# Threshold attention and a bilinear feed-forward layer on one core: the turned weights cross DRAM by head and partition

## The chip, the cores and the metric

The kernel runs on one core of one Trainium2 chip. The metric is the device time of an execution in microseconds. A core has five engines, each with its own instruction stream: TensorE (PE in the profile) multiplies matrices and writes to PSUM, VectorE (DVE) and ScalarE (ACT) do the elementwise work, GpSimd (POOL) does more of it on SBUF alone, and SyncE (SP) issues DMA transfers. Sixteen DMA engines carry the transfers between DRAM and SBUF; SBUF has 128 partitions.

## The reference

Attention first, for 8 batches and 8 heads, 576 positions, 64 features per head, all in fp32:

```python
scores = np.matmul(q, k.transpose(0, 1, 3, 2)) / sqrt(64)
thresh = np.max(scores, axis=-1, keepdims=True) - tau
scores = np.where(scores >= thresh, scores, -1e9)
attn = softmax of scores along the keys          # written out with max, exp, sum
x = np.matmul(attn, v)                           # then (B, H, S, D) -> (B*S, H*D) = (4608, 512)
out = ((x @ w_a) * (x @ w_b)) @ w_out            # d_ff = 1536
```

So a weight of a query is nonzero only where its score lies within tau of the maximum of its row. The weights are multiplied with v, and for that product the keys must lie on the partitions, whereas the softmax needs the queries on the partitions. The kernel therefore has to turn every matrix of weights.

## The kernel before

**Tiling.** Work is done in pairs of heads (32 pairs, index `i`, four pairs to a batch) and units (index `u`): units 0 to 3 hold 128 queries each for both heads of the pair, unit 4 holds the last 64 queries of two neighbouring pairs. There are 144 units. One turn of the outer loop, called a slot below, starts one unit and moves earlier ones along: scores (line 404, PE), maximum and threshold (411, 412, DVE), exponential (432, ACT), mask and sum (435, DVE), normalising (454, ACT), turning, and three slots after its scores the product with v (542, PE).

**Turning.** The first eight units are turned on PE. All others go through DRAM. `turn_blocks` lets DVE transpose the tile `tw`, 128 queries by 2 heads by 576 keys, in blocks of 32 by 32 (line 498, one instruction for each head, 128x576). After that, partition g\*32+p of `tw` holds key p of each of the 18 key blocks, for the 32 queries of group g. The block groups still have to move to other partitions, and four DMAs per unit, one for each group g of 32 partitions, write them to a DRAM scratch tile `swap` (runs of 1,152 bytes, 144 KB each). One slot later `turn_back` reads `swap` into the tile `wT` with two DMAs of 288 KB, each for two of the groups and all 128 partitions, in runs of 1,152 bytes. A unit 4 has eight writes of 72 KB. The product (`weighted`, `product`) then multiplies `wT` with `vm`, the rows of v: partition by partition, slot s by slot s, so that v must be laid out over partitions and slots as the keys of `wT` are.

**Loads of v.** `load_v` brings v of one pair. For pairs from the second batch on it posts four DMAs of 72 KB, each to 32 partitions. For the first four pairs v is loaded at the start in one order and once more, with `again`, in the order that the turned weights need.

**Order of the work.** The order on every engine is fixed when the program is written. The feed-forward layer (lines 720 and 824 for the two input products, 885 and 935 for the output) is a generator whose matmuls fill the slots; `advance` takes a number of columns from it, and how much each slot takes follows from the backlog. All these transfers are issued by SP, in order, each behind the waits of those ahead of it. Up to slot 36 `post` issues a transfer at once (line 144). From then on it is put into a list, `bulk`, the transfers of turned weights ahead of recent loads. `passed` takes entries from that list as PE's columns go by (320 columns for each 144 KB) and issues them at line 157; the first move of such an entry waits for the PE instruction last written before it. `flush` issues, without that wait, everything up to an entry that is about to be needed. `load_weights` (line 271) brings the weights of the layer in the first 120 us.

Three buffers hold `tw` (`TW_BUFS`), five scratch tiles in DRAM each hold `swap` for units 0 to 3 and for unit 4, and `wT` has two buffers of one unit each (`bufs=2`), so that a read into `wT` has to wait until the product before the last has used its buffer.

Of the kernel before, what the change touches and what calls it, by code (L numbers as in the profile page):

```python
# [10 lines left out]
FP32 = mybir.dt.float32  # L11
# [43 lines left out]
def kernel(  # L55
# [39 lines left out]
    B, H, S, D = q.shape  # L95
    P = 128
    Q = 32
    DM = H * D
    DFF = w_a.shape[1]
    HP = H // 2  # L100
    NT = 4
# [3 lines left out]
    NB = S // Q  # L105
# [6 lines left out]
    NSLOT = 9  # L112
    G = P // Q
# [4 lines left out]
    def pool(name, bufs, **kw):  # L118
        return ctx.enter_context(tc.tile_pool(name=name, bufs=bufs, **kw))
# [5 lines left out]
    scratch = pool("scratch", 5, space=bass.MemoryType.DRAM)  # L125
# [9 lines left out]
    loaded = {}  # L135
# [3 lines left out]
    def post(key, *moves):  # L139

        if not state["paced"]:
            for move in moves:
                state["turn"] += state["over"]
                (nc.scalar if state["turn"] % 2 else nc.sync).dma_start(*move)  # L144
        else:
            at = len(bulk)
            if key[0] in ("tw", "wT"):
                while at and bulk[at - 1][0][0] not in ("tw", "wT") and bulk[at - 1][1] >= state["slot"] - 1:
                    at -= 1
            bulk.insert(at, (key, state["slot"], moves))  # L150
# [13 lines left out]
    def flush(*keys):  # L164

        while any(key in keys for key, _, _ in bulk):
            pump(1, False)
# [33 lines left out]
    def load_v(i, again=False):  # L201
        b, hp = pairs[i]
        if not again:
            loaded[i]["v"] = loads.tile([P, NSLOT, D], FP32, tag="vm", bufs=HP, name="vm")
        for j in range(2):
            rows, half = v[b, 2 * hp + j], loaded[i]["v"][j * D:(j + 1) * D]
            if i >= HP or again:
                if i < HP:
                    rows = rows.rearrange("(c s p) d -> p c s d", c=2, p=Q)
                else:  # L210
                    rows = rows.rearrange("(p c s) d -> p c s d", c=2, p=Q)
                post(("v", i), *((half[c * Q:(c + 1) * Q], rows[:, c]) for c in range(2)))
            else:
                nc.sync.dma_start(half, rows.rearrange("(s p) d -> p s d", p=D))

# [10 lines left out]
    for f in range(NG):  # L226
        for c in range(HP):
            for dst, w in ((wa_sb, w_a), (wb_sb, w_b)):
                src = []
                for r in range(2):  # L230
                    chunks = [(2 * c + e) % HP * 2 + (r + (c >= HP // 2)) % 2 for e in range(2)]
                    cols = slice(f * CW + r * CH, f * CW + (r + 1) * CH)
                    rows = w[:, cols].bitcast(U32).rearrange("(k p) f -> p k f", p=D)
# [98 lines left out]
    for _ in range(TW_BUFS):  # L332
        t = work.tile([P, 2 * NB, Q], FP32, tag="tw", bufs=TW_BUFS, name="rows")
# [10 lines left out]
    load_rows(2, "k", rooms[5])  # L344
    load_weights(RAWS)
    load_v(0)
    load_rows(3, "q", rooms[6])
    load_rows(3, "k", rooms[7])
# [6 lines left out]
    prepared, scored, weights, turned, whole = {}, {}, {}, {}, {}  # L355
    x_of, xtail_of = {}, {}
    ahead, settled, settled_of = {}, {}, {}
    blocks, complete, swaps = [], [], {}
# [106 lines left out]
    def turned_tile():  # L465
        return work.tile([P, G + 1, NSLOT, Q], FP32, tag="wT", bufs=2, name="wT")
# [26 lines left out]
    def turn_blocks(i, u):  # L493

        ws, _ = weights.pop((i, u))
        t = whole.pop((i, u))
        for w in ws:
            nc.vector.transpose(w, w)  # L498
        swap = scratch.tile([G, P, NSLOT * Q], FP32, tag="swap" if u < NT else "swapt", name="swap")
        swaps[i, u] = swap  # L500
        for g in range(G):
            if u < NT:
                moves = [(swap[g].rearrange("(r p) e -> p r e", p=Q),
                          t[g * Q:(g + 1) * Q].rearrange("p (r s) e -> p r (s e)", r=G))]
            else:
                moves = []
                for m in range(2):
                    j = g // 2 ^ m
                    moves.append((swap[2 * m + g % 2, j * D:(j + 1) * D].rearrange("(r p) e -> p r e", p=Q),
                                  t[g * Q:(g + 1) * Q, m * NB:(m + 1) * NB].rearrange("p (r s) e -> p r (s e)", r=2)))  # L510
            post(("tw", i, u), *moves)

    def turn_back(i, u):

        key = "wT", i, min(u // 2, 1) if i >= HP else u // 2
        if u < NT or i < HP:
            flush(("tw", i, u))
            swap = swaps.pop((i, u)).rearrange("g p e -> p g e")
            turned[i, u] = turned_tile()
            for y in range(0, G, 2):  # L520
                post(key, (turned[i, u][:, y:y + 2].rearrange("p g s e -> p g (s e)"), swap[:, y:y + 2]))
        if i >= HP and u == (3 if i % 2 else NT):
            flush(("tw", i - i % 2, NT))
            swap = swaps[i - i % 2, NT].rearrange("g p e -> p g e")
            for y in range(2):
                post(key, (turned[i, 2 + y][:, G].rearrange("p s e -> p (s e)"), swap[:, i % 2 * 2 + y]))
            if i % 2:
                del swaps[i - 1, NT]
# [506 lines left out]
    first = {i: g for g, (i, u) in enumerate(units) if u == 0}  # L1035
# [21 lines left out]
    n = 0  # L1057
# [4 lines left out]
    for g in range(len(units) + PV_LAG):  # L1062
# [9 lines left out]
        if BY_PE + 1 < g <= len(units) + 1:  # L1072
            n = g - PV_LAG
            back = (1 if BY_PE <= n and parts(*units[n]) else 0,)
            if not back[0]:
                turn_back(*units[g - 2])
        if here:
            i, u = units[g]
# [20 lines left out]
        if g > BY_PE and g <= len(units):  # L1099
            turn_blocks(*units[g - 1])  # L1100
# [19 lines left out]
        if g > BY_PE:  # L1120
            n = g - PV_LAG
            held = 0.0
            now = parts(*units[n]) if BY_PE <= n < len(units) else []
            if now:
                held = 384 - (PORTIONS[2] + PORTIONS[3]) * pace + NSLOT * sum(width(*x) for x in now) // 2
                held = min(max(held, 0.0), 384)
            advance(PORTIONS[1] * pace - held)
            for p, h in now:
                if pairs[p][1] == 0:
                    make_x(2 if h == 1 and p >= HP and pairs[p][0] % GT == 0 else 1)  # L1130
                make_room()
                weighted(p, h)
                passed(NSLOT * width(p, h) // 2)
                running["owed"] -= NSLOT * width(p, h) // 2
            if back and back[0] > 0:
                turn_back(*units[g - 2])
# [21 lines left out]
        for p in range(1, NPR):  # L1158
            if g == first[p] - 1:
                load_v(p)  # L1160
        if BY_PE <= g < BY_PE + HP:
            load_v(g - BY_PE, again=True)
# [63 lines left out]
```

## Time and profile before

| | |
|---|---|
| runs, median of 3 | 1419.77 us (1418.38 to 1431.88) |
| profiled execution, span from first to last instruction | 1417.0 us |
| profiled execution, own time | not printed; the fastest run is 1.4 us and the median 2.8 us above the span |
| granted TensorE clock, mean | 0.994 |
| PE busy | 1370.2 us (97%) |
| DVE busy | 1013.7 us (72%) |
| ACT busy | 679.9 us (48%) |
| POOL busy | 495.7 us (35%) |
| SP's DMA queue, all transfers | 323,712 packets, 216.95 MB, 59.2% of 16 engines' time |
| of these, writes of `swap` | 480 of 144 KB (2.9 us to landing), 128 of 72 KB (3.0 us) |
| of these, reads into `wT` | 244 of 288 KB (3.9 us), 56 of 144 KB (3.3 us) |
| of these, loads of `vm` after the start | 128 of 72 KB (2.5 us) |

The busy share of an engine is an average over the whole span. The page also gives the span in forty slices; the trace can be asked for any stretch, for what each engine waited for, and for the chain of work that ended last. "Landing" is the time from SP's issue of a transfer to the semaphore that tells of its last byte. Where the page names a line, it is a line of the kernel printed above; an arrow `wT<-swap` reads "written from".

### The profile page before, as it was taken

The page shows a single profiled execution, that of the slowest core. Times are in us where ns is not written, and L with a number is a line of the kernel's source. Part 1 is how long each engine was busy: PE and PEld are TensorE (multiplying, and loading weights), DVE is VectorE, ACT ScalarE, POOL GpSimd, SP SyncE. Part 2 cuts the span into 40 slices and gives each one's busy share as a digit, 9 for nine tenths or more (in the row PEclk, how much of TensorE's full clock was granted, in tenths as well). Part 3 has the DMA queues.
Part 4 walks back from the last instruction along what each step waited for, and adds up shares of the span by engine and source line. Part 5 has one row for each costly group of instructions (what it writes and reads, how often), then busy time and mean ns, then how long its engine had stood idle before and what let it go on. Part 6 is the DMA issues. An engine that isn't in the chain of part 4 may idle for free.

```text
span 1417.0 us, 76257 instructions
## 1 busy us (share of the span) xinstructions
PE 1370.2 (97%) x33836; PEld 1229.6 (87%) x33836; DVE 1013.7 (72%) x2200; ACT 679.9 (48%) x1245; POOL 495.7 (35%) x678
## 2 busy tenths in 40 slices
PE   6788999999999999999999999999999999999998
PEld 5677579989878887979998999999888899799997
DVE  6898986778777877776767777677777776744424
ACT  5786554545445454545444545454545455431110
POOL 2674541606060606042333324150606060608100
PEclk9999999999999999999999999999999999999999
DMA  9967776667756775666555675567655775550000
GB/s 212 235 193 219 182 214 163 178 153 183 198 135 173 198 188 155 178 156 184 142 134 149 168 193 158 144 160 199 168 144 152 191 201 154 135 152 18 4 19 18
DMA packets 327000, 223.20 MB, mean 158 GB/s; under 512 B 171536, under 2 KB 310800, under 8 KB 326672
## 3 DMA queue, kind: packets, MB, share of 16 engines
q1 hardware_dynamic: 323712, 216.95, 59.2%
q8 instruction: 266, 4.36, 1.3%
q10 hardware_dynamic: 2960, 1.38, 0.4%
q14 instruction: 62, 0.51, 0.1%
HBM read 128.58 MB, written 89.65 MB: 154 GB/s over the span
## 4 chain that ended last, share of the span: by engine, by line
PE 86%; DVE 7%; DMA 3%; issue 2%; SPq 1%; ACT 0%; POOL 0%; DVEq 0%; POOLq 0%; ACTq 0%
PE pab L720 29%; PE po L885 20%; PE pab L824 16%; PE pv L542 10%; PE sc L404 10%; DVE mx L411 2%; DVE tw L498 2%; SPq L144 1%; DMA wT<-swap 1%; DVE tw L435 1%; PE tp L479 1%; DMA raw<-in_moe_w_a_dram 1%; DMA raw<-in_moe_w_b_dram 1%; DVE thr L412 0%; DVE u L790 0%
## 5 line engine op out<-in xcount | busy, mean ns | idle before, releaser
L411 DVE TENSOR_REDUCE mx<-sc 128x1 f32<-128x576 f32 x288 | 204.7, 752 | 125.8 <-PE sc L404 125.4
L454 ACT ACTIVATE tw<-tw,rcp 128x576 f32<-128x576 f32 x272 | 196.5, 770 | 202.3 <-DVE rcp L448 202.3
L682 POOL TENSOR_TENSOR h<-h,u 128x512 f32<-128x512 f32 x28 | 35.2, 1276 | 601.0 <-DVE h L794 426.1
L432 ACT ACTIVATE tw<-sc,bias,scalars 128x576 f32<-128x576 f32 x288 | 239.8, 833 | 10.9 <-PE pab L720 0.4
L435 DVE SCALAR_TENSOR_TENSOR tw<-sc,thr,tw 128x576 f32<-128x576 f32 x288 | 221.5, 799 | 10.4 <-ACT tw L432 9.9
L885 PE MATMUL po<-wo_sb,h 64*64 64x256 f32 x3264 | 205.8, 376 | 1.2 <-DVE h L794 1.1
L498 DVE STREAM_TRANSPOSE tw<-tw 128x576 f32<-128x576 f32 x272 | 194.4, 752 | 0.8 <-ACT tw L454 0.8
L885 PEld LDWEIGHTS po<-wo_sb,h 64*64 64x64 f32 x3264 | 157.0, 133 | 25.7 <-DVE h L794 2.6
L542 PE MATMUL pv<-wT,vm 64*64 64x160 f32 (+3 forms) x5184 | 169.2, 275 | 7.6 <-issue 3.6
L542 PEld LDWEIGHTS pv<-wT,vm 64*64 64x64 f32 x5184 | 157.4, 136 | 19.1 <-issue 9.8
L404 PE MATMUL sc<-kT,qT 64*64 64x288 f32 x2016 | 168.0, 404 | 1.1 <-DVE xt L550 0.5
L853 POOL TENSOR_TENSOR h<-h 128x256 f32<-128x256 f32 x168 | 117.4, 732 | 107.4 <-PE po L885 97.2
L885 PE MATMUL po<-sums_u,h 64*64 64x256 f32 x2448 | 153.4, 376 | 0.7 <-DVE h L832 0.7
L720 PE MATMUL pab<-xU,wb_sb 64*64 64x128 f32 x4352 | 138.0, 269 | 0.4 <-issue 0.3
L720 PEld LDWEIGHTS pab<-xU,wb_sb 64*64 64x64 f32 x4352 | 132.2, 133 | 3.7 <-issue 1.1
L885 PEld LDWEIGHTS po<-sums_u,h 64*64 64x64 f32 x2448 | 117.6, 133 | 19.4 <-DVE h L832 1.3
L404 PEld LDWEIGHTS sc<-kT,qT 64*64 64x64 f32 x2016 | 101.8, 133 | 22.6 <-issue 5.0
L549 ACT COPY xT<-pv 128x128 f32<-128x128 f32 (+1 forms) x68 | 17.7, 260 | 201.8 <-PE pv L542 200.2
L431 ACT ACTIVATE bias<-mx,scalars 128x1 f32<-128x1 f32 x288 | 83.1, 288 | 64.0 <-DVE mx L411 63.7
L550 DVE COPY xT<-pv 64x128 f32<-64x128 f32 (+1 forms) x136 | 38.1, 280 | 91.0 <-PE pv L542 89.7
L720 PE MATMUL pab<-xS,wa_sb 64*64 64x128 f32 x2176 | 101.8, 269 | 0.1
L531 ACT COPY kept<-po 128x512 f32<-128x512 f32 x65 | 34.8, 536 | 123.0 <-PE po L885 113.9
(156 smaller groups left out, 2414.3 us busy)
## 6 DMA issues: line engine op xcount, KB each, us to landing
wT<-swap SPq DMA_DIRECT2D x244, 288.0 KB, 3.9
swap<-tw SPq DMA_DIRECT2D x480, 144.0 KB, 2.9
vm<-in_v_dram SPq DMA_DIRECT2D x128, 72.0 KB, 2.5
swap<-tw SPq DMA_DIRECT2D x128, 72.0 KB, 3.0
kT<-in_k_dram SPq DMA_DIRECT2D x112, 72.0 KB, 3.3
wT<-swap SPq DMA_DIRECT2D x56, 144.0 KB, 3.3
out_dram<-kept SPq DMA_DIRECT2D x28, 256.0 KB, 3.9
qT<-in_q_dram SPq DMA_DIRECT2D x112, 40.0 KB, 2.8
```

Source lines behind the costliest of these rows:

```text
L404: nc.tensor.matmul(sc[m][o * D:o * D + wide, c], qT[r, q0:q0 + wide], kT[r, c * SH:(c + 1) * SH], start=True, stop=True)
L411: nc.vector.tensor_reduce(mx[:, c], sc[j], axis=AX.XY, op=ALU.max)
L431: nc.scalar.activation(bias[:, j:j + 1], mx[:, j:j + 1], AF.Copy, scale=e_nscale)
L432: nc.scalar.activation(wb[j], sb[j], AF.Exp, bias=bias[:, j:j + 1], scale=e_scale)
L435: nc.vector.scalar_tensor_tensor(out=wv, in0=sb[j], scalar=thr[:, j:j + 1], in1=wv, op0=ALU.is_ge, op1=ALU.mult, accum_out=sums[:, j:j + 1])
L454: nc.scalar.activation(w, w, AF.Copy, scale=rcp[:, j:j + 1])
L498: nc.vector.transpose(w, w)
L542: nc.tensor.matmul(pv[c * D:(c + 1) * D, y], vm[rows, s], wT[y](rows, s), start=(s == 0), stop=(s == NSLOT - 1))
L720: nc.tensor.matmul(out[c * D:(c + 1) * D, r, f * P:(f + 1) * P], w[g][k][rows, w0:w0 + D], moving[k][rows], start=(fresh and k == 0 and f ...
L824: nc.tensor.matmul(pab[c:c + columns(), r], w[rows, f // n, k, fs + c:fs + c + columns()], moving, start=(k == 0), stop=(k == H - 1))
L853: (nc.vector if state["over"] else nc.gpsimd).tensor_tensor(*a, **kw)
L885: nc.tensor.matmul(po[c * D:(c + 1) * D, r, y], ht[rows, t0:t0 + D], other[rows, f], start=(f == 0), stop=(f == NF // 2 - 1))
```

## The change

The turned weights of units 0 to 3 are written to DRAM by head: `swap` becomes two blocks of 128 partitions by 576 values, and one DMA for each head writes what each partition holds of that head as one run of 2,304 bytes. Each of the two reads then fetches one head: it fills 64 partitions (head 0 the lower ones, head 1 the upper) for all four groups, still in runs of 1,152 bytes, because the two halves of a partition's run (c = 0 and 1) go to neighbouring partitions. A key that lay on partition c\*32+p of its half now lies on p\*2+c. Unit 4 is written with four DMAs in place of eight, each with two runs of 2,304 bytes for a partition, to places in DRAM that lie interleaved; it is read as before.

The loads of v follow the new order of the keys. For pairs from the second batch on, each partition then needs one run of 2,304 bytes, and the pair is loaded by one DMA of 288 KB over 128 partitions. The second load of the first four pairs keeps its four DMAs, each to every other partition of a half.

```diff
-            if i >= HP or again:
-                if i < HP:
-                    rows = rows.rearrange("(c s p) d -> p c s d", c=2, p=Q)
-                else:
-                    rows = rows.rearrange("(p c s) d -> p c s d", c=2, p=Q)
-                post(("v", i), *((half[c * Q:(c + 1) * Q], rows[:, c]) for c in range(2)))
+            if again:
+                rows = rows.rearrange("(c s p) d -> p c s d", c=2, p=Q)
+                post(("v", i), *((half[c:D:2], rows[:, c]) for c in range(2)))
+            elif i >= HP:
+                if j == 0:
+                    both = v[b, 2 * hp:2 * hp + 2].rearrange("j (q s) d -> (j q) (s d)", s=NSLOT)
+                    post(("v", i), (loaded[i]["v"].rearrange("p s d -> p (s d)"), both))
...
-        swap = scratch.tile([G, P, NSLOT * Q], FP32, tag="swap" if u < NT else "swapt", name="swap")
+        if u < NT:
+            swap = scratch.tile([2, P, S], FP32, tag="swap", name="swap")
+            for j in range(2):
+                post(("tw", i, u), (swap[j], t[:, j * NB:(j + 1) * NB].rearrange("p n e -> p (n e)")))
+        else:
+            swap = scratch.tile([G, P, NSLOT * Q], FP32, tag="swapt", name="swap")
+            rows = swap.rearrange("g (j p c) x -> (g j) p (c x)", j=2, c=2)
+            for g in range(G):
+                first, step = 2 * (g % 2) + g // 2, 5 - 2 * (g // 2)
+                post(("tw", i, u), (rows[first:first + step + 1:step].rearrange("m p x -> p m x"),
+                                    t[g * Q:(g + 1) * Q].rearrange("p (m n) e -> p m (n e)", m=2)))
         swaps[i, u] = swap
-        for g in range(G):
-            if u < NT:
-                moves = [(swap[g].rearrange("(r p) e -> p r e", p=Q),
-                          t[g * Q:(g + 1) * Q].rearrange("p (r s) e -> p r (s e)", r=G))]
-            else:
-                moves = []
-                for m in range(2):
-                    j = g // 2 ^ m
-                    moves.append((swap[2 * m + g % 2, j * D:(j + 1) * D].rearrange("(r p) e -> p r e", p=Q),
-                                  t[g * Q:(g + 1) * Q, m * NB:(m + 1) * NB].rearrange("p (r s) e -> p r (s e)", r=2)))
-            post(("tw", i, u), *moves)
...
-            swap = swaps.pop((i, u)).rearrange("g p e -> p g e")
+            swap = swaps.pop((i, u))
             turned[i, u] = turned_tile()
-            for y in range(0, G, 2):
-                post(key, (turned[i, u][:, y:y + 2].rearrange("p g s e -> p g (s e)"), swap[:, y:y + 2]))
+            for y in range(2):
+                if u < NT:
+                    rows, groups = slice(y * D, (y + 1) * D), slice(0, G)
+                    src = swap[y].rearrange("(g p) (c x) -> (p c) g x", g=G, c=2)
+                else:
+                    rows, groups = slice(0, P), slice(2 * y, 2 * y + 2)
+                    src = swap[groups].rearrange("g p e -> p g e")
+                post(key, (turned[i, u][rows, groups].rearrange("p g s e -> p g (s e)"), src))
```

## The prediction

> **What bounds the kernel now.** I read the page's busy times, slices and chain first, then PE's waits, then stretches of time, and last the transfers one by one.
>
> From the page of before (busy us by engine; the slices of PE and of the DMA engines; the shares of the chain that ended last):
>
> ```profile
> PE 1370.2 (97%) x33836; PEld 1229.6 (87%) x33836; DVE 1013.7 (72%) x2200; ACT 679.9 (48%) x1245; POOL 495.7 (35%) x678
> ...
> PE   6788999999999999999999999999999999999998
> ...
> DMA  9967776667756775666555675567655775550000
> ...
> PE 86%; DVE 7%; DMA 3%; issue 2%; SPq 1%; ACT 0%; POOL 0%; DVEq 0%; POOLq 0%; ACTq 0%
> ```
>
> PE is the bound. It idles for 35.2 us between its first and last matmul (gaps between successive matmuls, added up), of which 18.2 us lie before 100 us, where eight units are turned on PE and no weights cross DRAM until about 91 us. The DMA engines are half to three quarters busy almost throughout, and yet transfers make 3% of the chain. The stretches tell where (start:end, length, then busy us of PE, PEld, DVE, ACT, POOL, the granted clock, DMA share, GB/s):
>
> ```profile
> 100.00:125.00 25.00, 20.11 (x304) 18.51 (x302) 23.60 (x51) 18.32 (x37) 12.64 (x14) 1.00 0.90 263
> 125.00:133.00 8.00, 6.23 (x155) 5.84 (x157) 3.95 (x13) 3.14 (x8) 1.69 (x2) 0.57 0.74 204
> 133.00:200.00 67.00, 65.48 (x1066) 43.50 (x1066) 61.20 (x132) 38.97 (x74) 39.79 (x30) 1.00 0.73 183
> 200.00:1400.00 1200.00, 1191.13 (x30786) 1087.08 (x30782) 839.27 (x1817) 544.21 (x978) 383.38 (x560) 1.00 0.57 151
> ```
>
> From 200 us on PE idles for 8.9 us in 1,200, and no wait on a transfer is among PE's waits there. Between 100 and 200 us it idles for 8.2 us, with the one wait on the turned weights (engine, line, releaser; us in total, times, longest):
>
> ```profile
> PE pv L542 <- DMA wT<-swap: 2.9, 1, 2.9
> ```
>
> That wait ends at 126.8 us. What PE and its clock did around it (length, PE busy, clock, DMA share, GB/s):
>
> ```profile
> 105.40:108.90 3.50, 2.14 (x33) 1.00 1.04 253
> 108.90:112.30 3.40, 2.02 (x36) 1.00 1.04 354
> ...
> 122.50:125.90 3.40, 1.34 (x13) 1.00 0.84 282
> 125.90:129.30 3.40, 2.53 (x96) 0.51 0.70 177
> 129.30:132.80 3.50, 3.50 (x69) 0.51 0.84 229
> ```
>
> After the stretch with 1.34 us of PE work the granted clock is halved for 6.8 us, which costs 3.4 us; after those with 2.14 and 2.02 us it is not. **Everything that faster transfers can give is thus near 120 to 200 us: the 2.9 us, the 3.4 us and some tenths, about 6.5 us or 0.5%.**
>
> **How near the rest is to waiting.** For each of the 64 products from `swap` I subtracted the landing of its last read into `wT` from the start of its first matmul. For those after 200 us this slack is 2.8 to 12.2 us, mostly 4 to 8. For the eight from 126 to 197 us it is -0.6 to 1.4 us (below zero where the first matmuls use a tile read earlier), but for one with 9.0. This is what a slower read eats into.
>
> **SP's issues.** The turned weights in SP's queue (ns min/median/max of an issue, first and last start):
>
> ```profile
> L157 SPq DMA_DIRECT2D swap<-tw x480: 302/393/2142, 324.1 to 1258.5; - x160
> L144 SPq DMA_DIRECT2D swap<-tw x128: 302/432/2436, 91.4 to 314.5; - x128
> ```
>
> Each of the 120 units through DRAM loses two writes (240), each of 16 units 4 loses four (64), each of 28 pairs loses three loads of v (84): 388 of SP's transfers. At 0.39 to 0.43 us each that is 160 us of SP time. From 200 us on SP waits for PE and DVE anyway, so it is worth nothing. From 90 to 200 us SP issues 150 transfers that take 82 us, in runs without a pause; 40 of them go, 17 us. The read PE waits for at 126.8 us is the pair issued at 120.6 and 121.2 us. Before it stand eight unit-4 writes, four loads of v and four writes. The last writes can't start before DVE's transposes (116.3 to 117.8 us), so only what follows counts: two writes and a little, after which the read is issued near 118.6 us, **2.0 us earlier**. Issues before the read landing at 178.8 us fall likewise: three of v, two of writes, 5 x 0.45 = 2.2 us.
>
> **The write.** In the trace's packet records, taken where only one tile's transfers were in flight, a packet of 1,152 bytes took 74.2 ns on average (median 79) when writing `swap` from 32 partitions, and 61.8 ns (median 51) when reading into all 128. A packet of 2,304 bytes from 128 partitions isn't in the trace: at least the 93 ns median of the 2,304-byte packets of `vm`, at most their mean over all, 129 ns (they go to 32 partitions). The nearest row is the store of `out` from 128 partitions, 94.6 ns for 2,048 bytes, thus 106 ns. For a unit: 512 x 74.2 / 16 engines = 2.37 us before, 256 x 106 / 16 = 1.70 us after (1.50 to 2.06), a gain of 0.7 us (0.3 to 0.9). The first head can also go before the second transpose has ended, 0.75 us sooner by the transposes' 754 ns; the unit is complete no sooner.
>
> **The read.** The 61,440 packets keep their size, but fill only half of the partitions at a time. Nearest row: the 74.2 ns of the writes from 32; bounds 61.8 (nothing changes) and 104 (95th percentile of those writes). A pair of reads costs 512 x (74.2 - 61.8) / 16 = 0.40 us more (0 to 1.35). The Trainium skill has a rule against this part: "SBUF — State Buffer", section "Door 1: The DMA port swizzle", says that what counts is how many of 16 ports the partitions reach, and that partitions 0 to 63 reach eight, no more than 0 to 31 do. By it, reads into halves would go at half rate, 32 packets x 51 ns more for each engine and pair, an estimate of 1.6 us from that page's halving and the 51 ns median, and the sum below would come out near nothing; the 79 against 51 ns in this trace agree in direction.
>
> **The sum for the DMA engines**: writes 5,167 us of engine time to 3,690 (69,632 x 74.2 ns against 34,816 x 106), reads up by 762. That is 715 of 22,672 us, three points of share, with bounds of 8 points either way. After 200 us nothing waits for it.
>
> **v.** One load of 288 KB for four of 72 KB: the same bytes, a slot ahead of use. The repeated load has the same packets to every other partition. Both at nothing, hidden by that slot; uncovered, each would cost its landing, 2.5 us. `passed` now takes 288 KB per entry, at 640 columns; the last piece of a unit is taken 320 columns earlier than now. Nothing.
>
> **Sum.** At 126.8 us: 2.0 us sooner by SP, 0.2 to 0.4 later by the read, so the wait falls from 2.9 to about 1.2 us. PE then works for about 3 us instead of 1.34 in 122.5 to 125.9, more than the 2.02 after which the clock stayed: another 3.4 us. That would be 5.1 us. But DVE is busy for 61.2 of the 67 us that follow (91%), so part of it comes back as waits for DVE; and seven thin products lose some tenths. I take **3 us** (bounds: a gain of 6.5; a loss of 7 x 1.35 plus one more halved clock, 3.4, which is 12.9). The profiled span would go from 1417.0 to 1414.0. A span lies 1.4 us under the fastest run and 2.8 under the median, and I carry the difference to the median: 1419.8 - 3 = 1416.8 us.
>
> **Rivals.**
> - *Reads become the bound of the thin stretch*, 0.2 of the chance: SP's gain doesn't reach the reads, since the two `wT` buffers hold them until a product ends, and each read lands up to 1.35 us later. Seven products and one halved clock: 1420 to 1433 us. Against: SP's runs without pause there, in which a read leaves sooner. The rule of the Trainium skill named above leads here.
> - *Slower by over 1%: false order among interleaved writes*, 0.08. The four new writes of a unit 4 go to interleaved blocks of DRAM. If the program orders transfers by the outer bounds of what they touch, each waits for the landing of the one before: 3 x 3.0 us with SP held, against 8 x 0.41 now, 5.7 us more in each of 16 units 4. Reads behind have 3 to 8 us of slack, so 1 to 2 us would reach PE each time, and the repeated loads of v, likewise interleaved, would hold SP 8 x 2.5 us at the thinnest place, of which I count half: 1419.8 + 16 x 1.5 + 10 = 1454 us. It decides once SP is held longer than the slack, about 4 us. Against: in the output product GpSimd (line 853) writes one interleaved half of `h` while PE reads the other with no such wait.
> - *Faster by over 1%*, 0.04: the 8.9 us after 200 us would have to go as well, 1404 us. They are waits on DVE and issue; nothing here touches them.
> - *The traffic doesn't get cheaper* (2,304 bytes cost 129 ns and reads 104): DMA share up by 8 points, hidden by the slack after 200 us. It is part of the first rival.
>
> **Numbers.** The forecast, a gain of 0 to 6.5 us, has 0.68. One per cent, 14.2 us, is about what a measurement of this kernel can tell from no change. Faster 0.04, within 1% 0.88, slower 0.08. The range goes from 1411 (the gain of 6.5 and two for the spread of the runs) to 1433 (the first rival's end).
>
> **What would show it.** Right: the wait at 126.8 us shorter or gone and the clock whole there; writes of 288 KB with packets near 106 ns; reads with packets above 62 ns; PE again idle for under 10 us after 200 us. Wrong: waits of PE line 542 on `wT` after 200 us, several writes of a unit 4 with issues of 3 us, or a clock halved in more places.

## The result and the profile after

The changed kernel takes 1427.94 us (median of 22 runs, 1422.44 to 1433.26) against 1420.79 us before (22 runs, 1414.55 to 1431.88). The ratio is 1.0056, with a 95% interval of 1.0042 to 1.0070: **slower by about 8 us**, where a gain of 3 us was forecast. By the bound of 1% it is "within 1%"; the time lies in the range given. The profiled executions differ by more than the medians: spans of 1430.5 us (own time 1432.69) and 1417.0 us, so that a difference in microseconds between the two traces is up to twice that of a typical pair of runs.

The page of after, with busy times, slices, queues of the DMA engines (packets, MB, share of 16 engines) and the chain:

```profile
PE 1372.3 (96%) x33836; PEld 1210.5 (85%) x33836; DVE 1012.6 (71%) x2200; ACT 678.9 (47%) x1245; POOL 495.4 (35%) x678
...
PE   6788999999999999999999999999999999999998
...
DMA  9967865658547755665546755567546665450000
...
q1 hardware_dynamic: 282688, 216.93, 57.2%
q8 instruction: 266, 4.36, 1.3%
...
PE 85%; DVE 8%; DMA 3%; issue 2%; ACT 1%; SPq 1%; POOL 0%; DVEq 0%; POOLq 0%; ACTq 0%
```

SP's queue has 41,000 packets fewer and two points less of the engines' time, where three were forecast; nothing on this page looks like a loss. The stretches (start:end, length, busy us of PE, PEld, DVE, ACT, POOL, clock, DMA share, GB/s) show where it is:

```profile
100.00:125.00 25.00, 20.42 (x331) 18.86 (x331) 23.61 (x51) 18.26 (x37) 12.63 (x14) 1.00 0.88 258
125.00:133.00 8.00, 7.81 (x182) 7.56 (x176) 7.26 (x19) 6.37 (x15) 3.51 (x5) 1.00 0.86 218
133.00:200.00 67.00, 63.78 (x1076) 42.81 (x1076) 60.80 (x129) 38.30 (x72) 37.82 (x28) 1.00 0.76 197
200.00:1400.00 1200.00, 1181.64 (x30404) 1060.14 (x30400) 825.60 (x1795) 540.35 (x972) 382.76 (x560) 1.00 0.56 150
```

From 125 to 133 us PE is now busy for 7.81 us at full clock, where it had 6.23 us at 0.57. From 200 us on it idles for 18.4 us in place of 8.9. PE's matmuls come in the same order in both kernels, so the n-th matmul of one trace can be set against the n-th of the other: matmul 1,800 is 4.4 us earlier after the change, the 3,000th (at 205 us) 2.7 us earlier, and from there on the changed kernel loses 14.8 us until matmuls at 1300 us, in some twenty jumps of 0.3 to 1.9 us, less what is won back between them.

PE's waits on "issue" from 200 us on (engine, line, releaser; us in total, times, longest), at the same two lines first before, then after. Lines 720 and 726 are the same line of the two kernels, as are 542 and 548:

```profile
PE pab L720 <- issue: 1.2, 3, 0.6
PE pv L542 <- issue: 1.2, 2, 0.7
```

```profile
PE pab L726 <- issue: 9.2, 13, 1.5
PE pv L548 <- issue: 3.1, 6, 0.7
```

"Issue" means that no semaphore ended the wait. No read into `wT` is among the waits of either. The longest one in PE's timeline of after (start, length, what, idle before):

```profile
1127.78 1.11 PE L726 MATMUL pab<-xU,first_u 64*64 64x128 f32 x27
1130.44 1.20 PE L726 MATMUL pab<-xU,first_u 64*64 64x128 f32 x34 [1.54 <-issue]
```

The wait falls between two matmuls of one row of matmuls with the same operands. What it waits for is in the page's third part: queue 8, "instruction", 266 transfers of 16,384 bytes. I numbered PE's records (matmuls, weight loads, its sequencer's waits) in the order of their starts: 68,191 in the changed kernel, which is 266 times 256 with 95 left over. In the changed kernel 14 of PE's gaps over 300 ns from 200 to 1300 us come before a record whose number leaves **193 when divided by 256**, and no other remainder comes more than once; in the kernel before, 3 do, with the same remainder. Each of these gaps ends 1.2 to 1.6 us after a transfer on queue 8 has landed: here it lands at 1128.86 us and PE goes on at 1130.44. So every 256 instructions PE needs the next 16 KB of its program, and in these places it has come too late. I call them the steps of the instruction stream. The idle time of PE at the steps (within two instructions of them, 200 to 1300 us) is 2.2 us before and 12.8 us after; all its other idle time there is 6.6 and 5.5 us.

On average a fetch starts 0.72 us after PE has passed a step in the kernel before, and 1.01 us in the changed kernel; it lands 1.83 and 2.15 us after that step, and nine in ten within 2.74 and 3.39 us. PE needs it for the next step. A row of matmuls of 128 columns runs through 256 instructions in about 3.5 us (27 ns for a matmul and its weight load), and needs the fetch more than 1.2 us before their end. That is the margin: some tenths of a microsecond, for a transfer that the page counts on the same 16 DMA engines (1.3% of their time) as all that SP issues (57.2%). In the changed kernel a fetch that starts while no transfer of SP's is in flight starts 0.39 us after the step; with reads and writes of `swap` in flight, 1.64 us.

### The profile page after: what moved, and what is told of

It is laid out like the page before. It is cut to its first block, busy times and chain, and to the rows that moved or that the text cites. A ratio compares the mean times of both kernels' runs of the same rounds, so it can differ in the third digit from the quotient of the medians.

```text
span 1430.5 us, 75362 instructions
## 1 busy us (share of the span) xinstructions
PE 1372.3 (96%) x33836; PEld 1210.5 (85%) x33836; DVE 1012.6 (71%) x2200; ACT 678.9 (47%) x1245; POOL 495.4 (35%) x678
## 3 DMA queue, kind: packets, MB, share of 16 engines
q1 hardware_dynamic: 282688, 216.93, 57.2%
## 4 chain that ended last, share of the span: by engine, by line
PE 85%; DVE 8%; DMA 3%; issue 2%; ACT 1%; SPq 1%; POOL 0%; DVEq 0%; POOLq 0%; ACTq 0%
PE pab L726 29%; PE po L891 20%; PE pab L830 15%; PE pv L548 10%; PE sc L405 10%; DVE mx L412 2%; DVE tw L499 1%; DVE tw L436 1%; DMA qT<-in_q_dram 1%; PE po L941 1%; DVE low L312 1%; DMA raw<-in_moe_w_b_dram 1%; DVE thr L413 1%; SPq L144 0%; DVE wa_sb L320 0%
## 5 line engine op out<-in xcount | busy, mean ns | idle before, releaser
L891 PEld LDWEIGHTS po<-wo_sb,h 64*64 64x64 f32 x3264 | 151.0, 133 | 32.7 <-DVE h L800 2.5
L891 PEld LDWEIGHTS po<-sums_u,h 64*64 64x64 f32 x2448 | 112.8, 133 | 25.7 <-DVE h L838 1.4
```

The costliest lines, as they stand in the source:

```text
L891: nc.tensor.matmul(po[c * D:(c + 1) * D, r, y], ht[rows, t0:t0 + D], other[rows, f], start=(f == 0), stop=(f == NF // 2 - 1))
```

## The experiments

Theory 1: the reads into half of the partitions hold up the fetches. Its rivals: theory 2, the writes of 288 KB in long runs do; theory 3, the load of v in one piece does. Each kernel was timed against the kernel before on the same chip, and profiled once. "Idle at the steps" is the figure just defined, from that one profile.

**Half reads alone.** In the kernel before, `turn_back`:

```diff
-            for y in range(0, G, 2):
-                post(key, (turned[i, u][:, y:y + 2].rearrange("p g s e -> p g (s e)"), swap[:, y:y + 2]))
+            for y in range(2):
+                if u < NT:
+                    rows = slice(y * D, (y + 1) * D)
+                    post(key, (turned[i, u][rows, 0:G].rearrange("p g s e -> p g (s e)"), swap[rows]))
...
```

> The kernel before, with one part of the change: the two reads of a unit each fill 64 partitions for four groups instead of 128 partitions for two. Writes and loads of v as before. Idle time of PE at the 16 KB steps of its instruction stream, 200 to 1300 us: 2.2 us before, 12.8 us after. Theory 1 (reads into half of the partitions hold up the instruction fetches): 1428 to 1435 us, this idle time 8 to 14 us, reads landing in 4.5 to 5 us. Theory 2 (writes of 288 KB in long runs do it) and theory 3 (the load of v in one piece does it): 1419 to 1423 us, idle time 2 to 4 us.

Measured: ratio 1.0107 (1.0081 to 1.0132), idle at the steps 14.5 us, reads landing in 4.8 us. Theory 1 holds, with idle time and time just above its ranges (the ratio makes 1436 us of the 1420.79), and the reads alone cost more than the whole change. PE's largest wait of this kernel from 200 us on, again at the line of the first feed-forward product:

```profile
PE pab L724 <- issue: 11.8, 19, 1.4
```

**The rest of the change without the half reads.** In the changed kernel:

```diff
-            swap = scratch.tile([2, P, S], FP32, tag="swap", name="swap")
-            for j in range(2):
-                post(("tw", i, u), (swap[j], t[:, j * NB:(j + 1) * NB].rearrange("p n e -> p (n e)")))
+            swap = scratch.tile([G, P, NSLOT * Q], FP32, tag="swap", name="swap")
+            for g in range(G):
+                post(("tw", i, u), (swap[g].rearrange("(j p c) x -> p j (c x)", j=2, c=2),
+                                    t[g * Q:(g + 1) * Q].rearrange("p (j n) e -> p j (n e)", j=2)))
...
-                if u < NT:
-                    rows, groups = slice(y * D, (y + 1) * D), slice(0, G)
...
+                rows, groups = slice(0, P), slice(2 * y, 2 * y + 2)
+                src = swap[groups].rearrange("g p e -> p g e")
```

> The changed kernel, but the four writes of a unit go by group of 32 partitions (144 KB each, runs of 2,304 bytes) and its two reads fill all 128 partitions for two groups, as before. Load of v in one piece, as after. Theory 1 (half reads): 1416 to 1421 us, idle time at the steps of the instruction stream 2 to 4 us, reads landing in about 3.9 us. Theory 2 (large writes in long runs): between, 1421 to 1426 us, since the runs are long but the pieces small. Theory 3 (v in one piece): 1426 to 1430 us.

Measured: ratio **0.9965** (0.9946 to 0.9983), idle at the steps 5.6 us. It is faster than before, with the lowest ratio of all the kernels tried, though the idle time is above the 2 to 4 us that theory 1 expected. The rest of the change, taken together, is a gain; with the half reads it is a loss. Which part of the rest brings the gain isn't shown by this run.

```profile
PE pab L723 <- issue: 4.8, 11, 0.8
```

**v in four pieces, in the changed kernel.**

```diff
-                if j == 0:
-                    both = v[b, 2 * hp:2 * hp + 2].rearrange("j (q s) d -> (j q) (s d)", s=NSLOT)
-                    post(("v", i), (loaded[i]["v"].rearrange("p s d -> p (s d)"), both))
+                rows = rows.rearrange("(q s) d -> q s d", s=NSLOT)
+                post(("v", i), *((half[c * Q:(c + 1) * Q], rows[c * Q:(c + 1) * Q]) for c in range(2)))
```

> The changed kernel with v of a pair loaded in four pieces of 72 KB, each to 32 partitions, as before. Theory 1 and theory 2: 1427 to 1431 us, idle time at the steps of the instruction stream 10 to 15 us as after. Theory 3 (v in one piece): 1417 to 1421 us, idle time 2 to 5 us.

Measured: ratio 1.0042 (1.0022 to 1.0062), idle at the steps 17.0 us, more than the 10 to 15 expected. Theory 3 falls.

**Short runs in small writes, in the changed kernel.**

```diff
-                post(("tw", i, u), (swap[j], t[:, j * NB:(j + 1) * NB].rearrange("p n e -> p (n e)")))
+                for c in range(2):
+                    post(("tw", i, u), (swap[j, :, c * NSLOT * Q:(c + 1) * NSLOT * Q],
+                                        t[:, j * NB + c * NSLOT:j * NB + (c + 1) * NSLOT].rearrange("p n e -> p (n e)")))
```

> The changed kernel with each write of 288 KB cut into two of 144 KB, in runs of 1,152 bytes from 128 partitions; reads into half of the partitions, as after. Theory 1 (half reads): 1427 to 1432 us, idle time at the steps of the instruction stream 9 to 14 us. Theory 2 (large writes in long runs): 1418 to 1423 us, idle time 2 to 5 us. Theory 3: 1426 to 1430 us.

Measured: ratio 1.0047 (1.0022 to 1.0073), idle at the steps 13.3 us. Theory 2 falls. What is left is the reads, and the question is what about them.

**The same reads over all partitions.** In the first experiment's kernel, the reads take every other partition:

```diff
-                    rows = slice(y * D, (y + 1) * D)
-                    post(key, (turned[i, u][rows, 0:G].rearrange("p g s e -> p g (s e)"), swap[rows]))
+                    post(key, (turned[i, u][y:P:2, 0:G].rearrange("p g s e -> p g (s e)"), swap[y:P:2]))
```

> As e1_half_reads, but the two reads of a unit take the even and the odd partitions instead of the lower and the upper half: again 64 partitions and four groups each, the same packets, but spread over all of SBUF's partitions. Theory A (what counts is which partitions a read reaches, so that packets to one half stand in each other's way): as before, ratio 0.998 to 1.004, reads of about 62 ns a packet, idle time at the steps of PE's instruction stream 2 to 6 us. Theory B (64 partitions by four groups is a bad shape in itself, by its rows in DRAM or its four rows for each engine): as e1_half_reads, ratio 1.008 to 1.013, about 74 ns a packet, idle time 10 to 17 us.

Measured: ratio 1.0053 (1.0032 to 1.0074), idle at the steps 4.2 us, 65.7 ns a packet. On the fetches theory A holds: 64 partitions spread over all of SBUF are as harmless as 128. But the time did not come back, and neither theory had that. VectorE's waits on transfers from 200 us on:

```profile
DVE kT L365 <- DMA kT<-in_k_dram: 8.3, 3, 3.9
DVE qT L365 <- DMA qT<-in_q_dram: 6.3, 6, 1.8
```

The loads of q and k, which stand last in SP's list, come late; VectorE, which turns them, holds up PE, in gaps of 3.0 and 3.4 us. A likely reason, not tested by itself, is in SP's own rows (ns min/median/max of an issue), of this kernel:

```profile
L157 SPq DMA_DIRECT2D swap<-tw x480: 302/397/2260, 325.7 to 1273.7; - x160
L157 SPq DMA_DIRECT2D wT<-swap x244: 343/580/1625, 322.5 to 1284.2; - x122
```

A read of 64 partitions by four groups takes SP 580 ns to issue. Before, a read of 128 partitions by two groups, with the same 256 runs, took 382. For 240 reads that is 47 us of SP. The half reads of the first experiment have it too (574 ns, and 12.1 us of waits on q and k), and so does the changed kernel, which makes up for it with the issues that it saves:

```profile
L157 SPq DMA_DIRECT2D wT<-swap x244: 325/574/1856, 319.3 to 1280.6; - x122
L157 SPq DMA_DIRECT2D swap<-tw x240: 302/345/2995, 323.1 to 1269.7; - x120
```

SP's total doesn't settle it: between 325 and 1260 us its issues take 578 us in the kernel before, 615 in this one and 603 in the full reads cut in two (below), whose waits on q and k are only 2.5 us.

**Quarter reads**, four of 32 neighbouring partitions, in the kernel before:

```diff
-            for y in range(2):
+            for y in range(G if u < NT else 2):
...
-                    rows = slice(y * D, (y + 1) * D)
+                    rows = slice(y * Q, (y + 1) * Q)
```

> As e1_half_reads, but four reads of 144 KB to 32 partitions each, four groups. Theory A with the rule of the Trainium skill (SBUF — State Buffer, Door 1: 32 neighbouring partitions reach as many ports as 64 of one half): as e1_half_reads, ratio 1.007 to 1.014, about 74 ns a packet, idle time 10 to 17 us; two more issues of SP a unit add 1 to 4 us between 90 and 200 us. A theory in which the rate falls with the number of partitions: packets of 90 ns or more, ratio over 1.018, idle time over 20 us.

Measured: ratio 1.0157 (1.0130 to 1.0183), idle at the steps 3.4 us, 70.3 ns a packet. Packets to 32 partitions, in reads of half the size, are not slower than those to 64 (74.2 ns), as the Trainium skill's "SBUF — State Buffer" has it in "Door 1: The DMA port swizzle"; but the fetches are not held up, against theory A. The loss is of the other kind: SP has 240 issues more, and VectorE waits 33.2 us for q and k.

**A slower pace**, in the changed kernel and in the one with reads over all partitions:

```diff
-PUMP = 320
+PUMP = 480
```

> The changed kernel with its transfers paced at 480 columns of PE for each 144 KB in place of 320, so that they come less densely. If the instruction fetches come late because transfers are queued ahead of them on the DMA engines: idle time at the steps of PE's instruction stream falls from 12.8 to 5 to 10 us, and the time from a ratio of 1.0056 to 0.999 to 1.004, unless reads then miss their products (waits of the product on the reads, which would show by name). If the fetches are late for a reason other than the queue: 12 to 15 us and 1.004 to 1.008.

> e2_group_runs (full reads, long runs by group, v in one piece) with its transfers paced at 480 columns in place of 320. By the queue theory idle time at the steps of the instruction stream falls from 5.6 to 2 to 4 us and the ratio from 0.9965 to 0.993 to 0.996. If the pace doesn't matter, 0.995 to 0.998; if reads then miss their products, above 0.998.

Measured: 1.0193 (1.0161 to 1.0225) and 1.0141 (1.0110 to 1.0173). Idle at the steps went from 5.6 to 2.0 us with the full reads, as expected of fewer transfers in the way, but only from 12.8 to 11.9 us with the half reads. That is next to the 12 to 15 us expected of a cause other than the queue, so how densely the transfers follow one another isn't what the half reads do their harm by. (The profile of 11.9 us is of the slowest of the six runs, 1462.84 us against a median of 1451.73.) What decides both times is something else: the loads of q and k, which come last, are now so late that VectorE waits 45.1 and 44.4 us for them. In the second of the two:

```profile
DVE kT L366 <- DMA kT<-in_k_dram: 30.6, 11, 4.8
DVE qT L366 <- DMA qT<-in_q_dram: 13.8, 9, 4.7
```

**Half reads cut in two.** In the changed kernel, four reads of 144 KB for a unit, to the same half of the partitions:

```diff
-            for y in range(2):
+            for y in range(G if u < NT else 2):
                 if u < NT:
-                    rows, groups = slice(y * D, (y + 1) * D), slice(0, G)
-                    src = swap[y].rearrange("(g p) (c x) -> (p c) g x", g=G, c=2)
+                    rows, groups = slice(y // 2 * D, (y // 2 + 1) * D), slice(y % 2 * 2, y % 2 * 2 + 2)
+                    src = swap[y // 2].rearrange("(g p) (c x) -> (p c) g x", g=G, c=2)[:, groups]
```

> The changed kernel with each read of 288 KB cut into two of 144 KB: the same 64 partitions, two of the four groups each, so the same packets and the same partitions, but 8 instead of 16 packets of one transfer on each DMA engine. Theory Q (a fetch of PE's instructions waits for one transfer's share of packets on its engine, so the length of that share counts: 16 x 51 ns before, 16 x about 90 after): idle time at the steps of PE's instruction stream falls from 12.8 to 2 to 6 us, ratio 0.994 to 1.001, if the two more issues of SP a unit don't make the loads of q and k late. Theory P (packets that go to one half of the partitions delay a fetch by their mere presence): 10 to 16 us, ratio 1.004 to 1.010.

Measured: ratio 1.0010 (0.9987 to 1.0034), idle at the steps 5.2 us, 66.2 ns a packet. Theory P falls: the same bytes to the same partitions don't hold up the fetches in pieces of half the size. Theory Q's numbers are met; the page's transfers (KB each, us to landing):

```profile
wT<-swap SPq DMA_DIRECT2D x536, 144.0 KB, 3.4
swap<-tw SPq DMA_DIRECT2D x240, 288.0 KB, 3.4
```

**One read of 576 KB**, in the kernel before:

```diff
-            for y in range(0, G, 2):
-                post(key, (turned[i, u][:, y:y + 2].rearrange("p g s e -> p g (s e)"), swap[:, y:y + 2]))
+            if u < NT:
+                post(key, (turned[i, u][:, 0:G].rearrange("p g s e -> p g (s e)"), swap))
...
```

> The kernel before with one read of 576 KB for a unit of 0 to 3 in place of two of 288 KB: all 128 partitions, four groups, 32 packets of one transfer on each engine. Theory Q: a share of 32 x 51 ns, as long as that of the half reads, so idle time at the steps of PE's instruction stream 8 to 16 us, ratio 1.004 to 1.012 (one issue less for SP may give 1 to 2 us back). Theory P: 2 to 5 us, ratio 0.996 to 1.002.

Measured: ratio 1.0010 (0.9987 to 1.0032), idle at the steps 5.6 us. Theory Q had 8 to 16 us for a share of 32 packets on each engine; it falls, or has to be limited to 16 packets.

**A faster pace** with the full reads:

```diff
-PUMP = 320
+PUMP = 260
```

> e2_group_runs with its transfers paced at 260 columns for each 144 KB in place of 320, so that they come more densely and the loads of q and k earlier. Expected by both theories: no waits of VectorE on loads of q and k (1.3 us in e2_group_runs), idle time at the steps of the instruction stream 5 to 9 us (5.6 in e2_group_runs), ratio 0.995 to 0.999.

Measured: ratio 0.9975 (0.9955 to 0.9995), idle at the steps 4.6 us, VectorE's waits on q and k 1.4 us. The same as with 320.

**One write of 576 KB**, in the kernel with cut reads, and **full reads cut in two**:

```diff
-            for j in range(2):
-                post(("tw", i, u), (swap[j], t[:, j * NB:(j + 1) * NB].rearrange("p n e -> p (n e)")))
+            post(("tw", i, u), (swap.rearrange("j p x -> p j x"), t.rearrange("p (j n) e -> p j (n e)", j=2)))
```

> e9_after_cut_reads with the two writes of a unit 0 to 3 joined into one of 576 KB from all 128 partitions: 16 packets of about 97 ns of one transfer on each engine, 1.55 us, without any crowding on one half of the partitions. Theory Q2 (a fetch waits for up to 16 packets of one transfer on its engine, so packet time times packets up to 16 counts: 16 x 51 for a read of before, 16 x 81 to 104 for a half read, 8 x 97 for a write of after): idle time at the steps of PE's instruction stream 9 to 15 us, ratio 1.003 to 1.010. Theory C (only packets that crowd on one half of the partitions hold a fetch up, and only if enough of them come at once): 3 to 7 us, ratio 0.996 to 1.002.

```diff
-            for y in range(2):
-                rows, groups = slice(0, P), slice(2 * y, 2 * y + 2)
+            for y in range(G if u < NT else 2):
+                rows, groups = slice(0, P), slice(y, y + 1) if u < NT else slice(2 * y, 2 * y + 2)
```

> e2_group_runs with each read of 288 KB cut into two of 144 KB, one group and 128 partitions each: 8 packets of 51 ns on each engine. Theory Q2: idle time at the steps of the instruction stream falls from 5.6 to 2 to 4 us; by theory C it stays at 4 to 6. In both, two more issues of SP a unit make the loads of q and k later (waits of VectorE on them 1.3 us in e2_group_runs, 3 to 15 here), ratio 0.996 to 1.004.

Measured: 1.0016 (0.9990 to 1.0042) with idle at the steps of 6.1 us, and 0.9991 (0.9971 to 1.0012) with 4.1 us. The long shares of the write, 16 packets of 97 ns, hardly add to the 5.2 us: theory Q2 falls, theory C stands. The 4.1 us lie where the ranges of the two theories meet and decide nothing; the cut full reads bring no gain in time.

All kernels side by side, from one profile each, in the order of idle time at the steps. "Fetch" is the time from a step until the next block has landed, within which nine in ten stay; packets of reads are means where only reads into `wT` were in flight; the last column is VectorE's waits on loads of q and k after 200 us.

| kernel | ratio | idle at the steps, us | fetch, us | read packet, ns | waits on q, k, us |
|---|---|---|---|---|---|
| full reads, pace 480 | 1.0141 | 2.0 | 2.76 | 66.6 | 44.4 |
| before | 1 | 2.2 | 2.74 | 61.8 | 7.8 |
| quarter reads | 1.0157 | 3.4 | 2.78 | 70.3 | 33.2 |
| full reads cut in two | 0.9991 | 4.1 | 2.89 | 64.4 | 2.5 |
| even and odd reads | 1.0053 | 4.2 | 3.01 | 65.7 | 14.9 |
| full reads, pace 260 | 0.9975 | 4.6 | 2.85 | 64.5 | 1.4 |
| after, half reads cut in two | 1.0010 | 5.2 | 2.88 | 66.2 | 6.0 |
| full reads, long runs by group | 0.9965 | 5.6 | 3.09 | 64.8 | 1.3 |
| one read of 576 KB | 1.0010 | 5.6 | 2.90 | 65.8 | 5.8 |
| cut reads, one write | 1.0016 | 6.1 | 2.79 | 66.7 | 9.2 |
| after, pace 480 | 1.0193 | 11.9 | 3.24 | 71.7 | 45.1 |
| after | 1.0056 | 12.8 | 3.39 | 72.1 | 1.0 |
| after, short runs | 1.0047 | 13.3 | 3.34 | 74.8 | 0.5 |
| before, half reads | 1.0107 | 14.5 | 3.37 | 74.2 | 12.1 |
| after, v in four | 1.0042 | 17.0 | 3.44 | 74.2 | 0.0 |

The two groups don't overlap: the five kernels with reads of 288 KB into one half have 11.9 to 17.0 us of idle time at the steps, all others 2.0 to 6.1. Within the others the single profiles can't rank kernels, and a few microseconds between them mean little.

## Why the prediction was wrong

The forecast was a gain of 3 us, the measurement a loss of 8. Step by step:

- **The wait at 126.8 us: as forecast in this profile, but the clock's part isn't shown to be the change's.** The wait was to fall from 2.9 to about 1.2 us and the clock to stay whole. The wait there is now 0.85 us (the read lands at 124.4 us, the product starts at 124.6), and the stretches (length, busy us as above, clock, DMA share, GB/s) have no halved clock:

```profile
122.50:125.90 3.40, 2.48 (x84) 1.99 (x80) 3.37 (x7) 3.33 (x8) 2.37 (x3) 1.00 0.42 151
125.90:129.30 3.40, 3.28 (x89) 3.14 (x91) 2.69 (x11) 1.83 (x7) 0.68 (x2) 1.00 0.88 282
```

The changed kernel at the slower pace issues the same transfers in the same order until 320 us. In its profile the wait is 1.9 us and the clock is halved for 6.8 us:

```profile
125.90:129.30 3.40, 3.11 (x133) 3.14 (x137) 2.44 (x7) 0.86 (x3) 0.62 (x1) 0.62 0.71 229
129.30:132.80 3.50, 3.50 (x34) 3.08 (x31) 1.47 (x5) 2.69 (x6) 0.94 (x2) 0.50 0.82 200
```

In the kernel before with half reads alone, which saves SP no issue, the wait is 2.3 us and the clock stays whole, after only 1.17 us of PE work in 122.5 to 125.9. So the clock at this place differs from one execution to the next, and the rule that the prediction read from three stretches isn't enough to tell when it is halved.

- **SP: right where it counted.** The pair of reads is issued at 119.0 and 119.5 us in place of 120.6 and 121.2, 1.6 us earlier against 2.0 forecast. Of the 4.4 us gained there in this profile (1.2 in that of the slower pace), 2.7 are left at 200 us; the forecast took 3 of 5.1. Missed: a half read takes SP 0.2 us longer to issue. Nor are the saved issues worth nothing after 200 us: VectorE's waits on q and k fall from 7.8 to 1.0 us.
- **Packets: right.** The write's packets take 97.0 ns (forecast 106, bounds 93 to 129), the half read's 72.1 (forecast 74.2). The write got cheaper, and the read lands in 4.8 us in place of 3.9. The share of SP's queue fell by 2.0 points, forecast three. The Trainium skill's rule on ports ("SBUF — State Buffer", "Door 1: The DMA port swizzle") was right about which reads slow down, as the even and odd partitions show with 65.7 ns, but not by its factor of two: 72.1 against 61.8 ns on average, with a median of 51 ns in both.
- **"After 200 us nothing waits for it": wrong.** This is the step that failed. It was drawn from the slack of the reads, and it is true of them: no product waits for `wT` after 200 us, before or after. But the reads are not the only ones to use the DMA engines. PE's own instructions come over them, 266 blocks of 16 KB, at a margin of tenths of a microsecond, and I had left out queue 8 of the page and, in the rival "faster by over 1%", had said of the waits on "issue" that nothing here touches them. In the trace of before two gaps, of 0.63 and 0.76 us, already stood at steps of the instruction stream, at 603 and 875 us. Another page of the Trainium skill describes the blocks: "Runtime: NRT & Kernel Launch", section "Instruction fetch mechanics", has an engine's program refilled in blocks of 16 KiB, 256 instructions, over a DMA queue of its own, which the 256 of this trace confirm. It also says that this is mostly hidden because instructions are dispatched more slowly than they are fetched. The trace of before agrees, with 2.2 us of 1,100. For a PE that gets through 256 instructions in 3.5 us beside half reads it is no longer so: 12.8 us here.
- **First rival: right cause, wrong place.** It gave the half reads 0.2, and 1420 to 1433 us, by seven late products before 200 us. The half reads are what costs, but after 200 us and by another way: the 1.7 us given back between 133 and 200 us are given back with full reads too (from 5.6 to 3.9). Where SP saves no issues, the rival's own mechanism does show: the kernel before with half reads alone has two waits of the product on `wT`, of 0.9 and 0.8 us at 176 us, a halved clock at 179 us, and 3.8 us lost there. That the measured 1427.94 us lies in this rival's range, and so in the whole range, is luck: its upper end comes from late products and a halved clock before 200 us, and the changed kernel's profile has no halved clock there and no product waiting for its reads but the first.
- **False order among interleaved writes: didn't happen.** The four writes of a unit 4 are issued 0.4 to 0.5 us apart (109.8 to 111.2 us), and the two repeated loads of v to every other partition follow each other in 0.65 us.
- **v at nothing: right**, as far as can be told: the changed kernels with v in one and in four pieces have 1.0056 and 1.0042, with intervals that overlap.

The 14.8 us that the profiled execution loses between 200 and 1300 us lie at the steps: adding up the differences between successive matmuls of the two traces, those within 24 instructions of a step of the changed kernel give 20.8 us, those near a step of the old one -4.5, the rest -1.5.

What stays open is why 288 KB into one half hold up a fetch and twice 144 KB don't. Neither the time of a transfer's packets on an engine (one read of 576 KB, one write of 576 KB) nor crowding on one half as such (cut reads, quarter reads) is enough; in these runs the harm came only with both. With the cut reads, SP needs 0.58 us to issue each piece, and packets are down to 66.2 ns, so it may be that the engines then never crowd; but no run here shows the engines one by one. How far the other 4 to 6 us of idle time at the steps could be brought down without making q and k late wasn't tried.

## What to carry to other kernels

When PE is busy for 99% of a stage, look for what feeds it besides data: waits on "issue" that recurred every 256 instructions were here its instruction fetches, and reads that no product waited for delayed them. Reads of 288 KB that fill only the lower or the upper half of the partitions cost more than the rest of the change brought; the version with runs of 2,304 bytes and reads over all 128 partitions kept a gain (0.9965). Where that gain comes from isn't shown. Long runs by themselves made no difference that the times can tell (1.0056 with them, 1.0047 without, half reads in both), and in the version that gains, a packet of 2,304 bytes written from 32 partitions takes 144.9 ns on average (where only these writes were in flight), about twice the 74.2 ns of 1,152 bytes before. And what stands last in a queue is what a slower pace hurts: here the loads of q and k, not the transfers that were changed.

## What the runs showed of the hardware that was not expected

- PE's instructions arrive in blocks of 16,384 bytes, one for every 256 instructions, in a queue that the page counts on the DMA engines that carry the data; in the changed kernel a fetch with reads and writes of `swap` in flight starts 1.64 us after a step, and 0.39 us with no transfer of SP's in flight. PE goes on 1.2 to 1.6 us after a late block has landed.
- Reads of 288 KB into 64 neighbouring partitions of one half came with 11.9 to 17.0 us of PE's idle time at these blocks in 1,100 us; with reads into 64 partitions spread over both halves, or cut into 144 KB, it was 4.2 to 6.1 us.
- SP takes 574 to 580 ns to issue a read of 64 partitions by four groups, and 382 ns for 128 partitions by two, with the same number of runs; 64 partitions by two groups, half the runs, still take 579 ns.
